# Sums of E and v of four tiles in one slot, heads visited 0 to 3 then 3 to 0 with four key buffers

## The chip, the cores and the metric

The kernel runs on one core of one Trainium2 chip. The metric is the device time of one execution in microseconds (us), lower is better. Before the change it is 1399.04 us, the median of 3 runs (1398.97 to 1399.08). The engines of a core run side by side, each through its own list of instructions, and wait for each other by semaphores: PE (matrix products; its weight loads stand as PEld), DVE (vector work), ACT (activations, copies out of PSUM), POOL (elementwise work on SBUF), SP (here it issues all DMAs).

## What is computed

Attention that keeps the 32 best keys of every query, and behind it a channel mix with the token before. In the reference, cut:

```python
# q, k, v: 8 batches, 8 heads, 576 tokens, 64 channels
scores = scale * np.matmul(q, k.transpose(0, 1, 3, 2))
kth = np.partition(scores, -32, axis=-1)[..., -32:-31]
scores = np.where(scores >= kth, scores, -1e9)
attn = np.exp(scores - scores.max(-1, keepdims=True))
attn = attn / (attn.sum(-1, keepdims=True) + 1e-09)
x = np.matmul(attn, v)            # heads side by side: 8, 576, 512
x_prev = ...                      # x, one token later
xk = mu_k * x + (1 - mu_k) * x_prev
xr = mu_r * x + (1 - mu_r) * x_prev
h = np.maximum(xk @ w_k, 0.0)     # 512 to 1024
out = sigmoid(xr @ w_r) * (h * h @ w_v)
```

## The kernel before

**Slots and visits.** Two heads lie side by side on the partitions as one pair (`hp`, four pairs a batch). A tile is 128 queries of one head against its 576 keys; a pair has nine tiles (the ninth holds the last 64 queries of both heads). The program is one long list of slots, one new tile a slot, 288 tiles in all; in one slot a tile gets its scores while older tiles are at later steps. `ORDER` gives the order of the steps within a slot, and it is the same in every slot. The tiles come in visits: for each batch the four pairs with tiles 0 to 3, then the four pairs again with tiles 4 to 8, each time in the order 0, 1, 2, 3.

**One tile.** In its own slot PE makes the scores (`ps`, L239; L243 for the ninth tile) and ACT copies them out (`keep`, L248). One slot later DVE looks for the best of seven pieces (`cand`, L272), two slots later it ranks them, ACT takes signs against a bound (L288) and POOL multiplies (L291), three slots later comes the threshold, exp (L299) and the masked E (L302). Four slots later PE transposes E (`turn_tile`, L318, and L328 for the last 64 keys) and ACT copies it out (`et`, `el`). Five slots later (`W = tiles[n - 5]`) comes `weigh`: the sums of E and v.

**The sums.** `weigh(g, U, u)` takes two tiles (one query block of both heads): eight products with `v_in` (L376) and two with `vr_in` (L378), and writes beside the scores in the same two PSUM banks. A unit `U` is four tiles. Before the change half u = 0 is weighed in the slot of the unit's second tile plus five, half u = 1 two slots later, when the unit is full; the ninth tile is weighed alone. In the slot of the full unit PE also transposes the inverse row sums (`turn_inverse`, L349), and one slot later DVE multiplies the sums by them into `xT` (`place`, L384, L389).

**Keys.** Each visit loads its keys by four DMAs (`load_keys`, tag `kt`, L179), turns them on PE by two groups of three transposes (`turn_k`, output `pk`, L208) and ACT copies each group out (`K`, L216), four and three slots ahead of the visit. `K` has two buffers. Queries come in the same way (`turn_q`: `pq`, L208, and `qs`, L211).

**The channel mix** is cut into pieces of twelve products (`ph`, `pz`, `pv`, L437 to L439; some have six), and a slot takes none, one or two of them in step `mix`, between `inv` and `weigh` on PE. How many is settled when the program is built, by a budget: each slot adds `PACE` = 4.60 to what is free on PE, at most `CAP` = 4.45, the steps take their planned costs off (`L.use("pe", ...)`), and a piece is placed while there is enough for it. Pieces also wait for tokens, that is for whole rows of `xT`. What is left over runs in slots behind the last tile.

```python
PACE, SHARE, PIECE, CAP, MOST = 4.60, 0.74, 1.52, 4.45, 2
            def inv():
                if W and (W.i % 2 or W.i == 8):
                    L.use("pe", 1.33 if W.i % 2 else 0.7)
            def weigh_():
                if W and (W.i % 2 or W.i == 8):
                    weigh(g, W.U, W.i // 2 % 2)
```

In the first some forty slots the weights of the channel mix are also loaded and split (`weight_block`), on DVE, ACT and POOL.

Of the kernel before, what the change touches and what calls it, by code (L numbers as in the profile page):

```python
# [21 lines left out]
HS = S // 2  # L22
# [10 lines left out]
NCH = 7  # L33
CUTS = [S * i // NCH for i in range(NCH + 1)]
# [10 lines left out]
def topk_attention_channel_mix(ctx: ExitStack, tc: tile.TileContext, q, k, v, mu_k, mu_r, w_k, w_v, w_r, out):  # L45
# [18 lines left out]
    el_hf = [consts.tile([128, 256], F32, name=f"el{i}") for i in range(2)]  # L64
# [31 lines left out]
    def weight_steps(g, L):  # L96

        blocks = [(w_r, wr, i, 0) for i in range(HP)]
        blocks += [(w_k, wk, i, c) for c in range(0, FF, 512) for i in range(HP)]
        blocks += [(w_v, wv, i, 0) for i in range(NFB)]  # L100
        for src, dst, i, c in blocks:
            weight_block(g, L, src[i * 128:(i + 1) * 128, c:c + 512], *(d[:, i, c:c + 512] for d in dst), half=dst is wv)
            yield
            yield

    def weight_block(g, L, block, hi, lo, half):
        val = g.one.tile([128, 512], U32, name="wval")
# [12 lines left out]
        st = g.one.tile([128, 512, 2], U32, name="wst")  # L120
        nc.sync.dma_start(st.rearrange("p c t -> p (c t)"), block.bitcast(U32))
# [3 lines left out]
        def magnitude():  # L125
            W.mag = g.one.tile([128, 512], U32, name="wmag")
            nc.scalar.activation(W.mag.bitcast(F32), high.bitcast(F32), AF.Abs)
# [72 lines left out]
    def new_k(g, P):  # L200
        P.K = g.two.tile([128, 2, HS], F32, name="K")
        P.qs = {}
# [107 lines left out]
    def turn_tile(g, T, L):  # L310
        U, i = T.U, T.i
        j, u = i % 2, i // 2 % 2
        if i % 4 == 0:
            U.et, U.el = {}, {}
        et = U.et[u, j] = g.two.tile([128, NKC, 128], F32, name=f"et{j}")
        pt = g.psT.tile([128, NKC, 128], F32, name="pt", tag="pm")
        for c in range(NKC):
            nc.tensor.transpose(pt[:, c, :], T.e[:, c * 128:(c + 1) * 128], ident)  # L318
        L.at(*EVAC, lambda: nc.scalar.activation(et, pt, AF.Copy))  # L319
        if i % 2 == 0:  # L320
            T.U.e0 = T.e
        if i % 2 or i == 8:
            es = (T.e,) if i == 8 else (T.U.e0, T.e)
            pl = extra(g)[:64, :len(es) * 128]
            el = U.el[u] = el_hf[g.turns % 2][:, :len(es) * 128]
# [328 lines left out]
    def prep_all(g, P, batch, hp, L):  # L654
        P.first, P.near = 0, False
# [27 lines left out]
    def new_batch(g):  # L683
        x = g.two.tile([128, HP, 1 + S], F32, name="xT")
        nc.vector.memset(x[:, :, 0:1], 0.0)
        return x

    def pipeline(g):
        L = Lanes()

        visits = [(b, hp, part) for b in range(B) for part in (range(4), range(4, 9)) for hp in range(HP)]
# [3 lines left out]
        where = [(p, i) for p, (*_, part) in enumerate(visits) for i in part]  # L695
        xT, tiles, state = {}, {}, {"tokens": 0, "wait": 0, "start": 0, "held": []}
# [62 lines left out]
        def new_pair(n):  # L759
# [3 lines left out]
            P.first, P.near = P.part[0], len(P.part) < 9  # L763
# [16 lines left out]
        while n < total + 7 or "next" in state or L.busy():  # L780
# [6 lines left out]
            def loads():  # L787
                for N, t in coming(n):
                    early = N.n > 1
                    if t == -5 or t == -4 and not early:  # L790
                        N.kt, N.qt = [load_keys(g, N.batch, N.hp, 0)], []
                    if t == -4:
                        N.kt.append(load_keys(g, N.batch, N.hp, 1))
                        if 8 in N.part:
                            N.rest = load_rest(g, N.batch, N.hp)
# [6 lines left out]
            def score():  # L802
                if n < total:
# [3 lines left out]
                    if i == P.first:  # L807
                        if p % HP == 0:
                            state["seen"] = g.two.tile([128, HP, 3, 9], F32, name="seen")
                        P.group, P.seen = state["seen"], state["seen"][:, p % HP]  # L810
# [15 lines left out]
            def inv():  # L826
                if W and (W.i % 2 or W.i == 8):
                    L.use("pe", 1.33 if W.i % 2 else 0.7)
# [15 lines left out]
            def weigh_():  # L844
                if W and (W.i % 2 or W.i == 8):
                    weigh(g, W.U, W.i // 2 % 2)

            def prep():
                for N, t in coming(n):
                    at = (-4, -3) if N.n > 1 else (-3, -2)  # L850
                    if t == at[0]:
                        new_k(g, N)
                    if t in at:
                        turn_k(g, N, at.index(t), L)
                    if t in (-2, -1):
                        turn_q(g, N, t + 2, L)
                    if t == 0 and 8 in N.part:
                        turn_rest(g, N, L)
                    if -4 <= t < 0:
                        L.use("pe", 0.35)  # L860
                        L.use("act", 0.4)
# [59 lines left out]
            def place_():  # L921
                T = tiles.get(n - 6)
                if T and ends(T):
                    U = T.U
                    if U.P.b not in xT:
# [4 lines left out]
                        xT[U.P.b] = new_batch(g)  # L930
                    U.xT = xT[U.P.b]
                    place(U)
                    if U.P.hp == HP - 1 and T.i == U.P.part[-1]:
                        state["tokens"] = U.P.b * S + (S if T.i == 8 else 256)
                if V and V.i == V.P.part[-1] and V.P.hp == HP - 1:
# [98 lines left out]
```

## Time and profile before

| | |
|---|---|
| median of 3 runs | 1399.04 us (1398.97 to 1399.08) |
| profiled execution, its own time | 1397.27 us |
| span of its instructions | 1395.5 us |
| PE busy | 1257.8 us, 90% |
| DVE busy | 1154.9 us, 83% |
| ACT busy | 1113.2 us, 80% |
| POOL busy | 910.3 us, 65% |
| HBM | 55 GB/s over the span |

The span runs from the first to the last instruction of the profiled execution; its own time is 1.8 us longer, and the median of the runs 1.8 us longer again. Busy time is time in which at least one instruction of the engine ran; a busy PE is not PE at its peak, since its products are pipelined. The shares are means over stages with different limits, so the rows below go by stages.

### The profile page before, as it was taken

To read this page: it belongs to the slowest core of one execution; us is meant where nothing else is said; L and a number is where in the kernel's file an instruction comes from. 1 tells how busy PE (TensorE), PEld (TensorE's weight loads), DVE (VectorE), ACT (ScalarE), POOL (GpSimd) and SP (SyncE) were. 2 spreads that over 40 slices of the span, in tenths; PEclk is the share of its full clock that TensorE was granted. 3 is DMA by queue.
4 is the path that set the end of the run, shared out by engine and by line. 5 is a ranking of instruction groups with operands and counts; after the bars stand their busy time and mean duration, and the time that the engine had idled before them with its cause. 6 is when DMAs were issued, how large, how long until landed. Compare 5 with 4: busy or idle time off the path is not lost.

```text
span 1395.5 us, 32734 instructions
## 1 busy us (share of the span) xinstructions
PE 1257.8 (90%) x9909; PEld 961.0 (69%) x9909; DVE 1154.9 (83%) x6448; ACT 1113.2 (80%) x2588; POOL 910.3 (65%) x839
## 2 busy tenths in 40 slices
PE   5665767999999999898999999999999998999997
PEld 3443645676867687675867787777868686768786
DVE  6999899888898888989888898888888889888400
ACT  5777877898888888879889898888888887888541
POOL 3657886567655855657658675776666656757562
PEclk9777997999999999999999999999999999999999
DMA  4333232222221222222221222122222122111000
GB/s 102 85 89 84 59 95 66 59 50 56 50 68 40 62 52 60 51 50 64 47 71 41 53 62 63 41 55 57 66 52 51 43 70 68 37 45 37 21 16 22
DMA packets 243815, 78.78 MB, mean 56 GB/s; under 512 B 236464, under 2 KB 236464, under 8 KB 243632
## 3 DMA queue, kind: packets, MB, share of 16 engines
q1 hardware_dynamic: 243632, 76.61, 22.7%
q8 instruction: 82, 1.34, 0.4%
q14 instruction: 101, 0.83, 0.2%
HBM read 67.11 MB, written 9.44 MB: 55 GB/s over the span
## 4 chain that ended last, share of the span: by engine, by line
PE 66%; DVE 14%; ACT 9%; POOL 7%; issue 2%; SPq 0%; DMA 0%; DVEq 0%; ACTq 0%; POOLq 0%
PE ps L239 9%; PE ps L376 8%; PE pt L318 8%; PE ph L438 5%; PE ph L437 5%; PE pv L439 5%; PE ph L439 5%; PE pv L437 4%; PE pv L438 4%; DVE E L302 2%; DVE cand L272 2%; POOL sg L291 2%; PE pz L437 2%; PE pz L439 2%; PE pz L438 2%
## 5 line engine op out<-in xcount | busy, mean ns | idle before, releaser
L291 POOL TENSOR_TENSOR sg<-sc,sg 128x576 f32<-128x576 f32 x288 | 413.8, 1437 | 413.7 <-ACT sg L288 345.4
L272 DVE MAX8 cand<-sc 128x8 f32<-128x82 f32 (+1 forms) x2016 | 469.9, 233 | 10.1 <-ACT sc L248 8.1
L248 ACT ACTIVATE sc<-ps 128x576 f32<-128x576 f32 x288 | 187.0, 649 | 155.8 <-PE ps L239 101.9
L910 DVE MAX8 top<-sg 128x8 f32<-128x576 f32 x288 | 218.1, 757 | 80.4 <-POOL sg L291 78.8
L239 PE MATMUL ps<-K,qs 64*128 64x288 f32 x1024 | 207.6, 484 | 48.8 <-DVE xT L384 28.7
L299 ACT ACTIVATE se<-sc,seen 128x576 f32<-128x576 f32 x288 | 213.9, 743 | 27.2 <-DVE wval L133 25.3
L302 DVE SCALAR_TENSOR_TENSOR E<-sc,seen,se 128x576 f32<-128x576 f32 x288 | 233.0, 809 | 0.9 <-PE ps L243 0.3
L288 ACT ACTIVATE sg<-sc,seen 128x576 f32<-128x576 f32 x288 | 222.1, 771 | 5.0 <-DVE seen L283 2.6
L318 PEld LDWEIGHTS pt<-ident,E 128*128 128x128 f32 x1152 | 126.3, 145 | 133.5 <-issue 92.0
L318 PE MATMUL pt<-ident,E 128*128 128x128 f32 x1152 | 196.9, 296 | 13.8 <-DVE E L302 11.9
L376 PE MATMUL ps<-et,v_in 128*64 128x128 f32 (+1 forms) x2560 | 174.5, 282 | 22.5 <-ACT sc L248 15.2
L376 PEld LDWEIGHTS ps<-et,v_in 128*64 128x64 f32 x2560 | 136.9, 145 | 65.0 <-ACT sc L248 20.9
L438 PE MATMUL ph<-xl,wk 128*128 128x256 f32 (+2 forms) x608 | 172.5, 284 | 8.5 <-POOL xl L433 8.5
L437 PE MATMUL ph<-xh,wk 128*128 128x256 f32 (+2 forms) x608 | 178.9, 294 | 1.5 <-ACT r L454 1.3
L275 DVE MAX8 top<-cand 128x8 f32<-128x56 f32 x864 | 177.0, 205 | 0.1
L319 ACT ACTIVATE et<-pt 128x512 f32<-128x512 f32 x288 | 169.4, 588 | 4.0 <-PE pt L318 4.0
L439 PE MATMUL ph<-xh,wk 128*128 128x256 f32 (+2 forms) x608 | 171.3, 282 | 0.0
L239 PEld LDWEIGHTS ps<-K,qs 64*128 64x128 f32 x1024 | 82.2, 196 | 104.4 <-issue 34.6
L439 PE MATMUL pv<-wv,hl 128*128 128x512 f32 (+1 forms) x296 | 118.5, 400 | 9.2 <-POOL hl L458 9.2
L437 PE MATMUL pv<-wv,hh 128*128 128x512 f32 (+1 forms) x296 | 125.5, 424 | 0.0
L438 PEld LDWEIGHTS ph<-xl,wk 128*128 128x128 f32 x608 | 116.6, 192 | 11.1 <-POOL xl L433 10.9
L437 PEld LDWEIGHTS ph<-xh,wk 128*128 128x128 f32 x608 | 116.3, 191 | 2.4 <-ACT r L454 1.6
(95 smaller groups left out, 2687.4 us busy)
## 6 DMA issues: line engine op xcount, KB each, us to landing
kt<-in_k SPq DMA_DIRECT2D x256, 72.0 KB, 2.2
q_near<-in_q SPq DMA_DIRECT2D x256, 64.0 KB, 2.1
v_in<-in_v SPq DMA_DIRECT2D x128, 128.0 KB, 2.5
out<-eb SPq DMA_DIRECT2D x35, 256.0 KB, 2.3
wst<-in_moe_w_k SPq DMA_DIRECT2D x8, 512.0 KB, 4.0
wst<-in_moe_w_v SPq DMA_DIRECT2D x8, 512.0 KB, 3.8
vr_in<-in_v SPq DMA_DIRECT2D x64, 32.0 KB, 2.3
wst<-in_moe_w_r SPq DMA_DIRECT2D x4, 512.0 KB, 4.0
```

The source lines that it names most:

```text
L239: nc.tensor.matmul(g.ps[:, e], lhsT=P.qs[j][h, c * 128:(c + 1) * 128], rhs=P.K[h, j], start=True, stop=True)
L272: nc.vector.max(T.cand[:, 8 * i:8 * i + 8], T.sc[:, CUTS[i]:CUTS[i + 1]])
L288: nc.scalar.activation(T.side, T.sc, AF.Sign, bias=T.under, scale=-BELOW, accum_out=T.cnt)
L291: nc.gpsimd.tensor_mul(T.side, T.sc, T.side)
L299: nc.scalar.activation(g.pe, T.sc, AF.Exp, bias=T.nb, scale=SCALE)
L302: nc.vector.scalar_tensor_tensor(T.e, T.sc, T.thr, g.pe, op0=OP.is_ge, op1=OP.mult, accum_out=T.rs)
L318: nc.tensor.transpose(pt[:, c, :], T.e[:, c * 128:(c + 1) * 128], ident)
L376: nc.tensor.matmul(pa[hs[j]], lhsT=P.v[:, j, c, :], rhs=ms[c][j], start=(c == 0), stop=False)
L437: nc.tensor.matmul(ps, lhsT=sh, rhs=mh, start=first, stop=False)
L438: nc.tensor.matmul(ps, lhsT=sh, rhs=ml, start=False, stop=False)
L439: nc.tensor.matmul(ps, lhsT=sl, rhs=mh, start=False, stop=last)
L910: nc.vector.max(M.top[:, 24:32], M.side)
```

## The change

- `weigh_` now acts only in the slot of a full unit (`last`), and then weighs both halves, one behind the other: twenty products in one slot where ten stood in each of two. The planned cost on PE goes from 1.33 in each of two slots to 2.5 in one. For that, the transposed E of the first tiles is held longer: `et` of even tiles has three buffers where it had two, `el` three where it had two.
- The second round of visits of a batch takes the pairs in the order 3, 2, 1, 0. `K` has four buffers of its own, and a visit whose pair is still held (`homes`, `N.own` false) takes that `K`: no loads, no transposes, no copies of keys in the second round.
- To make room, the working tiles of the weight loading become parts of one tile, `early`, in the place of the odd batches' `xT`.
- Where the code asked for the fourth pair it now asks for the last visit of a round (`P.last`).

The diff, cut to what the steps below speak of:

```diff
+KEYS = 4
-    el_hf = [consts.tile([128, 256], F32, name=f"el{i}") for i in range(2)]
+    el_hf = [consts.tile([128, 256], F32, name=f"el{i}") for i in range(3)]
...
+        g.early = g.one.tile([128, HP * (1 + S)], F32, name="early", tag="x1")
...
-        val = g.one.tile([128, 512], U32, name="wval")
+        val = g.early[:, 1024:1536].bitcast(U32)
...
     def new_k(g, P):
-        P.K = g.two.tile([128, 2, HS], F32, name="K")
-        P.qs = {}
+        P.K = g.one.tile([128, 2, HS], F32, name="K", tag=f"K{P.home}")
...
-        et = U.et[u, j] = g.two.tile([128, NKC, 128], F32, name=f"et{j}")
+        et = U.et[u, j] = (g.two if j else g.three).tile([128, NKC, 128], F32, name=f"et{j}")
...
-        visits = [(b, hp, part) for b in range(B) for part in (range(4), range(4, 9)) for hp in range(HP)]
+        visits = []
+        for b in range(B):
+            visits += [(b, hp, range(4)) for hp in range(HP)]
+            visits += [(b, hp, range(4, 9)) for hp in reversed(range(HP))]
...
+        homes, held = {}, [(-1, None)] * KEYS
+        for p, (b, hp, part) in enumerate(visits):
+            home = next((h for h, (_, of) in enumerate(held) if of == (b, hp)), None)
+            own = home is None
+            if own:
+                home = held.index(min(held, key=lambda x: x[0]))
+            held[home] = p, (b, hp)
+            homes[p] = own, home
...
+            P.own, P.home = homes[n]
+            if not P.own:
+                P.K = next(N.K for N in reversed(Ps.values()) if (N.b, N.hp) == (P.b, P.hp) and N is not P)
...
-                    if t == -5 or t == -4 and not early:
-                        N.kt, N.qt = [load_keys(g, N.batch, N.hp, 0)], []
+                    if N.own and (t == -5 or t == -4 and not early):
+                        N.kt = [load_keys(g, N.batch, N.hp, 0)]
                     if t == -4:
-                        N.kt.append(load_keys(g, N.batch, N.hp, 1))
+                        N.qt = []
+                        if N.own:
+                            N.kt.append(load_keys(g, N.batch, N.hp, 1))
...
             def inv():
-                if W and (W.i % 2 or W.i == 8):
-                    L.use("pe", 1.33 if W.i % 2 else 0.7)
+                if last:
+                    L.use("pe", 2.5 if W.i < 8 else 0.7)
...
             def weigh_():
-                if W and (W.i % 2 or W.i == 8):
-                    weigh(g, W.U, W.i // 2 % 2)
+                if last:
+                    for u in range(2 if W.i < 8 else 1):
+                        weigh(g, W.U, u)
...
-                    if t in at:
+                    if N.own and t in at:
                         turn_k(g, N, at.index(t), L)
+                        L.use("pe", 0.35)
+                        L.use("act", 0.4)
                     if t in (-2, -1):
                         turn_q(g, N, t + 2, L)
+                        L.use("pe", 0.35)
+                        L.use("act", 0.4)
                     if t == 0 and 8 in N.part:
                         turn_rest(g, N, L)
-                    if -4 <= t < 0:
-                        L.use("pe", 0.35)
-                        L.use("act", 0.4)
```

How the order of instructions moves, at three places. Line numbers of the changed program are one or two higher for the same code.

First, PE in the slot of the last tile but one of a visit in the second round of batch 5 (the scores of tile 204), before the change. `px` from E are the last 64 keys of E, `px` from `rb` is the inverse, `pq` are queries; the twelve rows of one mix piece are left out behind its first three.

```order
L239 MATMUL ps<-K,qs_14397 128x288 x2
L318 MATMUL pt<-ident,E 128x128 x4
L328 MATMUL px<-ident,E 64x128
L208 MATMUL pq<-ident,q_near 128x128 x2
L349 MATMUL px<-ident,rb 128x128 x2
L437 MATMUL ph<-xh,wk_66 128x256
L438 MATMUL ph<-xl,wk_66 128x256
L439 MATMUL ph<-xh,wk_67 128x256
...
L376 MATMUL ps<-et_14523,v_in 64x128
L376 MATMUL ps<-et_14612,v_in 64x128
...
L378 MATMUL ps<-el_76,vr_in 64x128 x2
```

The same slot of the changed program: no mix piece stands in it, and the sums of both halves follow the inverse directly.

```order
L240 MATMUL ps<-K,qs_13956 128x288 x2
L319 MATMUL pt<-ident,E 128x128 x4
L329 MATMUL px<-ident,E 64x128
L209 MATMUL pq<-ident,q_near 128x128 x2
L350 MATMUL px<-ident,rb 128x128 x2
L377 MATMUL ps<-et_13947,v_in 64x128
L377 MATMUL ps<-et_14019,v_in 64x128
...
L379 MATMUL ps<-el_75,vr_in 64x128 x2
L377 MATMUL ps<-et_14083,v_in 64x128
L377 MATMUL ps<-et_14158,v_in 64x128
...
L379 MATMUL ps<-el_76,vr_in 64x128 x2
```

The piece has moved to an earlier slot, where one half of the sums stood before.

Second, PE in the slot before (tile 203), before the change, up to the first product of the mix: the keys of the next visit, `pk`, are turned here.

```order
L239 MATMUL ps<-K,qs_14332 128x288 x2
L318 MATMUL pt<-ident,E 128x128 x4
L328 MATMUL px<-ident,E 64x128 x2
L208 MATMUL pk<-ident,kt_14534 128x96 x3
L437 MATMUL ph<-xh,wk_66 128x256
```

The same place after the change; the next visit is of a pair whose keys are held, and the mix follows the transposes of E at once.

```order
L240 MATMUL ps<-K,qs_13888 128x288 x2
L319 MATMUL pt<-ident,E 128x128 x4
L329 MATMUL px<-ident,E 64x128 x2
L438 MATMUL ph<-xh,wk_66 128x256
```

Third, SP's queue near the end, in the second round of the last batch, before the change: `v_in` and `vr_in` of a visit, then keys (`kt`), the ninth tile's queries (`qr_in`) and the near queries of the next one.

```order
L194 DMA v_in<-in_v 128x4x64 x2
L195 DMA vr_in<-in_v 64x2x64
L179 DMA kt_20127<-in_k 96x3x64 x2
L179 DMA kt_20193<-in_k 96x3x64 x2
L186 DMA qr_in<-in_q 64x64 x4
L173 DMA q_near<-in_q 128x2x64 x4
```

And after the change: the four key loads are gone from the queue, the rest stands in the same order.

```order
L196 DMA v_in<-in_v 128x4x64 x2
L197 DMA vr_in<-in_v 64x2x64
L188 DMA qr_in<-in_q 64x64 x4
L175 DMA q_near<-in_q 128x2x64 x4
```

## Rows read from the trace of the kernel before

**Rows 1.** The page: busy time, share of the span and number of instructions of each engine, and the busy share of PE, DVE and ACT in 40 equal slices of the span (9 is 90% or more), with the granted clock of TensorE in tenths.

```profile
PE 1257.8 (90%) x9909; PEld 961.0 (69%) x9909; DVE 1154.9 (83%) x6448; ACT 1113.2 (80%) x2588; POOL 910.3 (65%) x839
...
PE   5665767999999999898999999999999998999997
...
DVE  6999899888898888989888898888888889888400
ACT  5777877898888888879889898888888887888541
...
PEclk9777997999999999999999999999999999999999
```

**Rows 2.** Busy time of each engine in three stretches of the span: the first 45 slots, the other 243 slots that have a tile, and the slots behind the last tile. Columns: stretch, its length, busy us of PE, PEld, DVE, ACT and POOL with their instructions, mean granted clock, DMA share, GB/s.

```profile
0.00:245.00 245.00, 163.40 (x1098) 114.04 (x1098) 219.81 (x1079) 179.45 (x392) 166.84 (x151) 0.83 0.33 83
245.00:1293.00 1048.00, 1003.22 (x8202) 771.62 (x8204) 917.24 (x5300) 897.21 (x2112) 693.10 (x632) 0.99 0.23 54
1293.00:1395.50 102.50, 91.18 (x616) 75.35 (x616) 17.81 (x72) 36.52 (x86) 50.37 (x57) 0.98 0.07 20
```

**Rows 3.** The same columns for two short stretches: three slots with no mix piece, and eleven slots with one or two each.

```profile
706.80:718.70 11.90, 9.09 (x79) 6.67 (x78) 11.64 (x67) 10.77 (x25) 8.66 (x8) 0.86 0.36 89
1033.70:1082.00 48.30, 48.30 (x400) 38.45 (x399) 41.28 (x239) 40.36 (x91) 31.13 (x29) 1.00 0.21 49
```

**Rows 4.** Groups of instructions over the whole span: line, engine, operation, out<-in, shapes, number | busy us, mean ns of one | idle time of the engine before them and what ended it. The transposes of keys, their copy by ACT, and the products of E and v. The last row is from the page's list of DMA issues: KB each and us to landing.

```profile
L208 PE MATMUL pk<-ident,kt 96*128 96x96 f32 x384 | 56.4, 257 | 8.3 <-DMA kt<-in_k 6.3 <-ACT wmag L127 1.4 <-ACT sc L248 0.2
L216 ACT ACTIVATE K<-pk 128x288 f32<-128x288 f32 x128 | 51.8, 405 | 2.4 <-PE pk L208 2.4
...
kt<-in_k SPq DMA_DIRECT2D x256, 72.0 KB, 2.2
```

**Rows 5.** The timeline of PE over two slots of the full stretch: start us, length us, engine, line, operation, out<-in, number, and idle time before it (none here). The products of the mix pieces are left out up to the last of each run.

```profile
915.64 0.40 PE L439 MATMUL pv<-wv,hl 128*128 128x512 f32 x1
915.97 1.09 PE L376 MATMUL ps<-et,v_in 128*64 128x128 f32 x16
916.89 0.39 PE L378 MATMUL ps<-el,vr_in 128*64 128x128 f32 x4
917.21 0.76 PE L239 MATMUL ps<-K,qs 64*128 64x288 f32 x4
917.90 0.66 PE L318 MATMUL pt<-ident,E 128*128 128x128 f32 x4
918.39 0.38 PE L328 MATMUL px<-ident,E 128*64 128x128 f32 x2
918.61 0.27 PE L208 MATMUL pr<-ident,qr_in 128*128 128x128 f32 x1
...
921.28 0.40 PE L439 MATMUL pv<-wv,hl 128*128 128x512 f32 x1
921.61 0.76 PE L239 MATMUL ps<-K,qs 64*128 64x288 f32 x4
922.29 0.66 PE L318 MATMUL pt<-ident,E 128*128 128x128 f32 x4
922.79 0.41 PE L208 MATMUL pk<-ident,kt 96*128 96x96 f32 x3
...
924.36 0.28 PE L439 MATMUL ph<-xh,wk 128*128 128x256 f32 x1
924.57 1.09 PE L376 MATMUL ps<-et,v_in 128*64 128x128 f32 x16
925.49 0.39 PE L378 MATMUL ps<-el,vr_in 128*64 128x128 f32 x4
925.81 0.76 PE L239 MATMUL ps<-K,qs 64*128 64x288 f32 x4
```

**Rows 6.** The timeline of all engines over the three slots without a mix piece of rows 3, same columns, cut to the scores (L239), ACT's copy of them (L248), the sums (L376) and DVE's `place` (L384).

```profile
706.84 0.76 PE L239 MATMUL ps<-K,qs 64*128 64x288 f32 x4
...
707.72 0.65 ACT L248 ACTIVATE sc<-ps 128x576 f32<-128x576 f32 x1 [1.46 <-PE ps L239]
...
708.58 1.09 PE L376 MATMUL ps<-et,v_in 128*64 128x128 f32 x16
...
709.82 0.76 PE L239 MATMUL ps<-K,qs 64*128 64x288 f32 x4
...
713.65 0.43 DVE L384 TENSOR_TENSOR xT<-ps,ri 128x256 f32<-128x256 f32 x1
...
714.13 0.76 PE L239 MATMUL ps<-K,qs 64*128 64x288 f32 x4 [2.50 <-DVE xT L384]
...
715.68 0.64 ACT L248 ACTIVATE sc<-ps 128x576 f32<-128x576 f32 x1
...
716.37 1.98 PE L376 MATMUL ps<-et,v_in 128*64 128x128 f32 x16 [0.31 <-ACT sc L248]
...
718.68 0.76 PE L239 MATMUL ps<-K,qs 64*128 64x288 f32 x4
```

**Rows 7.** The two longest of PE's waits between 245 and 1293 us: engine, its tile and line, what it waited for: us in total, times, longest us.

```profile
PE ps L239 <- DVE xT L384: 10.4, 5, 2.7
PE ps L376 <- ACT sc L248: 9.8, 11, 1.5
```

More of the change, by code (lines that the diff above doesn't have):

```diff
@@ L119, in weight_block @@
             return
-        st = g.one.tile([128, 512, 2], U32, name="wst")
-        nc.sync.dma_start(st.rearrange("p c t -> p (c t)"), block.bitcast(U32))
+        st = g.early[:, :1024].bitcast(U32).rearrange("p (c t) -> p c t", t=2)
+        nc.sync.dma_start(g.early[:, :1024].bitcast(U32), block.bitcast(U32))
         low, high = st[:, :, 0], st[:, :, 1]
@@ L125, in magnitude @@
         def magnitude():
-            W.mag = g.one.tile([128, 512], U32, name="wmag")
+            W.mag = g.early[:, 1536:2048].bitcast(U32)
             nc.scalar.activation(W.mag.bitcast(F32), high.bitcast(F32), AF.Abs)
@@ L324, in turn_tile @@
             pl = extra(g)[:64, :len(es) * 128]
-            el = U.el[u] = el_hf[g.turns % 2][:, :len(es) * 128]
+            el = U.el[u] = el_hf[g.turns % 3][:, :len(es) * 128]
             g.turns += 1
@@ L654, in prep_all @@
     def prep_all(g, P, batch, hp, L):
-        P.first, P.near = 0, False
+        P.first, P.near, P.home, P.qs = 0, False, 0, {}
         new_k(g, P)
@@ L681, in prep_first, with new_batch @@
         return lambda: half(1)
-    def new_batch(g):
-        x = g.two.tile([128, HP, 1 + S], F32, name="xT")
+    def new_batch(g, b=0):
+        x = g.one.tile([128, HP, 1 + S], F32, name="xT", tag=f"x{b % 2}")
         nc.vector.memset(x[:, :, 0:1], 0.0)
@@ L762, in new_pair @@
             P.b, P.hp, P.part = visits[n]
-            P.first, P.near = P.part[0], len(P.part) < 9
+            P.first, P.near, P.qs = P.part[0], len(P.part) < 9, {}
+            P.last = n % HP == HP - 1
+            P.own, P.home = homes[n]
+            if not P.own:
+                P.K = next(N.K for N in reversed(Ps.values()) if (N.b, N.hp) == (P.b, P.hp) and N is not P)
             P.batch = lambda x, b=P.b: x[b]
@@ L809, in score @@
                             state["seen"] = g.two.tile([128, HP, 3, 9], F32, name="seen")
-                        P.group, P.seen = state["seen"], state["seen"][:, p % HP]
+                        P.group, P.seen = state["seen"], state["seen"][:, P.hp]
                     if i % 4 == 0:
@@ L850, in prep @@
                     at = (-4, -3) if N.n > 1 else (-3, -2)
-                    if t == at[0]:
+                    if N.own and t == at[0]:
                         new_k(g, N)
-                    if t in at:
+                    if N.own and t in at:
                         turn_k(g, N, at.index(t), L)
+                        L.use("pe", 0.35)
+                        L.use("act", 0.4)
                     if t in (-2, -1):
                         turn_q(g, N, t + 2, L)
+                        L.use("pe", 0.35)
+                        L.use("act", 0.4)
                     if t == 0 and 8 in N.part:
                         turn_rest(g, N, L)
-                    if -4 <= t < 0:
-                        L.use("pe", 0.35)
-                        L.use("act", 0.4)
             def norm():
@@ L929, in place_ @@
                             L.force(g.read)
-                        xT[U.P.b] = new_batch(g)
+                        xT[U.P.b] = new_batch(g, U.P.b)
                     U.xT = xT[U.P.b]
                     place(U)
-                    if U.P.hp == HP - 1 and T.i == U.P.part[-1]:
+                    if U.P.last and T.i == U.P.part[-1]:
                         state["tokens"] = U.P.b * S + (S if T.i == 8 else 256)
-                if V and V.i == V.P.part[-1] and V.P.hp == HP - 1:
+                if V and V.i == V.P.part[-1] and V.P.last:
                     o = slice(V.P.first, V.i + 1)
```

## The prediction

> **What bounds the kernel now.** I begin with the busy shares and the slices of the page [rows 1]. PE leads with 90%, but its slices stand at 5 to 7 tenths for the first seventh of the span, while DVE's are full there, and at 9 after it. So I cut the span in three [rows 2]. In the first 245 us (45 slots, in which the weights are split) DVE is busy 219.8 and PE 163.4: PE is not the limit. From 245 to 1293 us (the other 243 slots with a tile) PE is busy 1003.2 of 1048.0, DVE 917.2, ACT 897.2. Behind that PE works off what is left of the mix.
>
> In the middle there are two kinds of stretch [rows 3]. Where slots hold mix pieces PE is busy 48.30 of 48.30 us, at full clock, and DVE 41.28. Where they hold none, DVE is busy 11.64 of 11.90 us and PE waits: three slots, so 3.88 us of DVE a slot. The timeline shows the first kind [rows 5]: the scores of successive tiles start at 917.21, 921.61 and 925.81, and what lies between is PE work without a gap. What a group costs PE is its end less the end of the group before it: scores 0.69, four transposes of E 0.59, the last keys' two 0.21, the transposes of keys 0.25 (922.79 + 0.41 against 922.29 + 0.66), two mix pieces 2.80 (918.88 to 921.68), one half of the sums 1.24 (916.04 to 917.28). They add up to the 4.40 and 4.20 us of the two slots. The second kind [rows 6]: slots of 2.98, 4.31 and 4.55 us, in which PE waits 2.50 us for `place`.
>
> So a slot costs about the larger of its PE work and DVE's 3.88. I put the group costs on the order of the program before, slot by slot. The 243 slots hold 980 us of PE work; taking 3.88 for every lighter slot gives 1038. The trace has 1048. The 10 left over I put down to the clock: its mean is 0.99 in that stretch [rows 2], and 1% missing at half speed is some 20 us at 1.2 GHz, in which up to half is lost. It shows in rows 6: after the wait of 2.50 us the sums take 1.98 where they took 1.09, and the granted clock of that stretch is 0.86 [rows 3].
>
> **The change part by part.**
>
> *Keys turned once.* 64 of 128 groups of transposes go, by the order 8 of 23 in the first 45 slots and 56 of 105 in the middle. A group costs PE 0.25 at least, and 56.4 us over 128 groups, 0.44, at most [rows 4], where nothing beside it overlaps; in a full stretch rows 5 are the case, and I take 0.26, which with the rest of the costs comes nearest to the slots. That is 56 x 0.26 = 14.6 us off PE in the middle. In the first 45 slots the 2 us off PE lie under DVE: 0, and 2 as a bound. ACT loses 64 copies of 0.405 us, 26 us [rows 4]; in full stretches ACT is busy 40.36 of 48.30 and hides them [rows 3], in light ones they could help DVE's chain a little: 0, bound 1. On SP 128 loads with 2.2 us to landing go [rows 4]; what stood behind them (queries, `qr_in`) is issued sooner, which nobody waits for in rows 7. The new `K` waits for the last scores of the pair that had its buffer, four visits back: 0.
>
> *Both halves of the sums in one slot.* The same twenty products run, 2 x 1.24 us, so nothing comes off. The first half moves two slots later on PE, past the scores, transposes and pieces of two slots; it issues no DMA. `et` and `el` have the buffers for it by the order (the third one is free when the next unit writes), and `place` still comes one slot after the second half. What was one slot of 4.2 and one of 4.5 becomes one with the sums and no piece (0.69 + 0.59 + 0.11 for one short transpose, 0.21 each for the pairs of the queries and the inverse, and 2.48: 4.29) and one with two pieces.
>
> *The mix.* By the order, 301 pieces stand in the middle before and 300 after, and 57 and 58 behind the last tile. Tokens come in the same slots, since the last visit of a round still ends the same slot. So the mix goes no earlier, and the work taken off PE partly becomes lighter slots. I did the same addition for the changed order: PE work 964 us (14.6 for the keys, 1.4 for the piece), and with 3.88 for each lighter slot 1029. Of the 16.0 us 7.0 are lost to slots in which DVE is the limit (58 us of such filling before, 65 after), and **9.0 us** come off.
>
> *The tail* has one piece more, 1.4 us, on a PE that is busy 91.18 of 102.50 us there: +1.4.
>
> *The clock.* By the order, runs of three or more slots in a row with less than 3.7 us of PE work number eight before and one after, which should leave fewer long waits; but single slots are down to 1.3 to 1.7 us after. Of the 10 us I take 1.5 as gained; bounds 0 and 10.
>
> *`early` in the place of `xT`.* By the order the last weight block is done in slot 41, and the tile of batch 1 is first written in slot 45: 0. If that cover were gone, `place` would wait on DVE for some slots, once.
>
> Sum: -9.0 + 1.4 - 1.5 = -9.1 us. The profiled execution took 1397.3 us by its own time (span 1395.5), and would take 1388.2; the median of the runs lies 1.8 above it, so **1390**.
>
> **The rivals.**
>
> *A: the idle time takes all of it.* The budget a slot (4.60) is unchanged, so full slots stay as long and the mix is only done sooner in each chunk. For it: 7 of 16 us go that way in my own sum. Against it: full slots have less in them (4.29 in the slots with sums, where they had up to 4.5). It gives 1399 + 1.4 - 1.5, within 0.2% of before (0.2%, 2.8 us, is about what a measurement of this kernel can tell from no change).
>
> *B: slower, by a wait of the sums for `keep`.* The sums write the banks from which ACT copies the scores, so they wait for that copy of the same slot [rows 7]. Before, a mix piece of 1.4 us mostly stood between. By the order 54 double sums stand right behind the inverse now, before only 21 single ones did. 11 waits took 9.8 us, 0.89 each [rows 7]. If as large a part of the 54 waits (28), that is 25 us: 1390 + 25 = 1415. It decides from 13 waits on (11.8 us, the gain and 0.2%). Behind a waiting product stand the next scores, and for them ACT and DVE. Against it: in rows 6 the copy of the scores that started at 706.84 ends at 708.37, 1.53 later, and the sums come 1.74 after them without a wait; the wait comes only where ACT was late itself (715.68, 1.55 after the scores), in a light stretch. The double sums stand at 1.8 in full ones. The Trainium skill (PSUM — Partial Sum Buffer, "PSUM bank collisions raise a hardware error") says that two engines may not touch one bank in the same partitions at once, whatever the columns, so this wait can't be dropped; the trace agrees, as these products do wait for a copy of other columns.
>
> *C: slower, by the clock.* The order after has 28 separate light runs where it had 22. In rows 6 a drop costs the sums 716.37 to 718.75, 2.38, instead of 1.24: 1.1 us and more. If each of the 28 brought one, 31 us instead of 10: 1412. Against it: PE falls to half in the rows only after a wait of 2.5 us, and single light slots are bridged, since DVE is ahead after full slots (41.28 of 48.30). The Trainium skill (TensorE: Matmul & The Clock Gate, "HAM oscillation — how this bites in real kernels") tells of just this: bursts with idle gaps between them start at half clock each time, which would make shorter, more frequent gaps a danger. Rows 3 and 6 agree that a gap is followed by half clock; how many of the new gaps are long enough no row shows.
>
> *D: more gain.* All 64 groups count, the filling doesn't grow and the half-clock time goes: -16.6 + 1.4 - 10, with the ACT bound 1373.
>
> **How the numbers follow.** The forecast (1383 to 1396) has 0.62, D 0.12, A 0.14, B 0.09, C 0.03. The range is to leave out B and C and the lower half of D: 1378 to 1400. Faster is the forecast and D, with a little added for A's lower edge: 0.75; same 0.14; slower B and C, 0.11.
>
> **What would show it.** `pk` x192 and `K` x64 in the groups; 28 us less of PE's summed products. From 245 us on, the last tile's scores about 9 us sooner. PE's busy time some 16 us less, its idle time some 6 more, most of it before scores that wait for `place`. The row of the sums waiting for `keep` should stay under 15 us; over 25 us means B. A mean clock under 0.98 in the middle means C. If the middle's slots start as late as before although PE is busy 15 us less, it is A. The prediction is wrong as a whole if full slots turn out longer than the sum of their groups, that is if three slots in a row with two pieces make ACT the late one.

## The result and the profile after

The changed kernel takes 1367.18 us, the median of four runs (1365.87 to 1370.06), against 1399.06 for the kernel before beside it: a ratio of 0.977, interval 0.976 to 0.979. That is 31.9 us off where 9 were forecast, and below the range. Both profiled executions can be compared line by line: 1397.3 us before (span 1395.5) and 1367.4 after (span 1365.6), 29.9 us apart. Of the other 2 us, 1.8 are the distance of the kernel before's profiled execution from its median.

The shares of the page after and the three stretches that answer to [rows 2], cut where slot 45 and the last tile start (columns as there):

```profile
PE 1229.5 (90%) x9717; PEld 947.6 (69%) x9717; DVE 1150.9 (84%) x6448; ACT 1096.0 (80%) x2524; POOL 908.5 (67%) x840
...
0.00:243.00 243.00, 164.78 (x1101) 115.80 (x1101) 222.33 (x1087) 179.86 (x389) 168.60 (x153) 0.82 0.32 78
243.00:1264.00 1021.00, 972.99 (x8002) 755.23 (x8004) 911.75 (x5299) 880.59 (x2051) 690.49 (x633) 0.99 0.20 47
1264.00:1365.60 101.60, 91.70 (x622) 76.54 (x621) 16.81 (x64) 35.56 (x84) 49.40 (x55) 0.98 0.07 20
```

The start is 5 us shorter (slot 45 begins at 242.9 instead of 247.8), the middle 24 (1020.9 instead of 1045.1, both from slot 45 to the last tile's scores), the tail 1. The groups that answer to [rows 4] and the waits that answer to [rows 7] (total us, times, longest):

```profile
L209 PE MATMUL pk<-ident,kt 96*128 96x96 f32 x192 | 28.7, 261 | 5.8 <-DMA kt<-in_k 5.2 <-ACT r L455 0.5
L217 ACT ACTIVATE K<-pk 128x288 f32<-128x288 f32 x64 | 25.9, 405 | 2.4 <-PE pk L209 2.4
...
PE ps L240 <- DVE xT L385: 10.7, 7, 2.1
PE ps L377 <- ACT sc L249: 7.0, 9, 1.3
```

Turns and copies of keys are halved as the diff says, and the sums wait less for `keep` than before, not more. Where the middle's 24 us went, by adding up PE's rows group by group (what each adds to the end of the one before it):

```
slots 45 to 287, us             before   after
PE work, all groups             1000.3   972.9
  transposes of keys              27.7    12.6
  sums                           158.9   151.9
  mix pieces (301, then 300)     432.6   427.3
PE waiting                        44.8    48.0
of it all, at 1.2 GHz             27.3    23.9
```

The keys are as forecast. The sums fell by 7 us though every product is still there (3200 rows of them in either trace). The timeline of PE in a slot with both halves, to be read against the single halves of [rows 5] (start us, length us, engine, line, operation, out<-in):

```profile
932.92 0.38 PE L350 MATMUL px<-ident,rb 128*128 128x128 f32 x2
933.23 1.09 PE L377 MATMUL ps<-et,v_in 128*64 128x128 f32 x16
934.16 0.39 PE L379 MATMUL ps<-el,vr_in 128*64 128x128 f32 x4
934.38 1.04 PE L377 MATMUL ps<-et,v_in 128*64 128x128 f32 x16
935.25 0.39 PE L379 MATMUL ps<-el,vr_in 128*64 128x128 f32 x4
935.57 0.72 PE L244 MATMUL ps<-K,qr 64*64 64x288 f32 x8
```

From a half's last group to what follows it takes 0.22 us where another half follows (934.16 to 934.38) and 0.32 where scores follow (935.25 to 935.57; in rows 5, 916.89 to 917.21). Over the slots of the middle at full clock the median half adds 1.243 us before, two side by side 2.334: 0.152 less than twice one half. What is saved is the way into the sums, not the way out: the scores behind them add 0.685 us (the median), and behind a mix piece 0.685 too.

### The profile page after: what moved, and what is told of

Its sections match the earlier page's. It is cut to its first block, busy times and chain, and to the rows that moved or that the text cites. A ratio compares the mean times of both kernels' runs of the same rounds, so it can differ in the third digit from the quotient of the medians.

```text
span 1365.6 us, 32014 instructions
## 1 busy us (share of the span) xinstructions
PE 1229.5 (90%) x9717; PEld 947.6 (69%) x9717; DVE 1150.9 (84%) x6448; ACT 1096.0 (80%) x2524; POOL 908.5 (67%) x840
## 4 chain that ended last, share of the span: by engine, by line
PE 65%; DVE 16%; ACT 10%; POOL 6%; issue 2%; SPq 0%; DMA 0%; DVEq 0%; ACTq 0%; POOLq 0%
PE ps L240 9%; PE ps L377 8%; PE pt L319 8%; PE ph L439 5%; PE ph L438 5%; PE ph L440 5%; PE pv L440 5%; PE pv L438 4%; PE pv L439 4%; DVE cand L273 3%; DVE E L303 3%; POOL sg L292 2%; ACT sg L289 2%; ACT sc L249 2%; PE pz L440 2%; PE pz L438 2%
## 5 line engine op out<-in xcount | busy, mean ns | idle before, releaser
L377 PEld LDWEIGHTS ps<-et,v_in 128*64 128x64 f32 x2560 | 142.9, 146 | 36.7 <-ACT sc L249 20.8
```

The costliest lines, as they stand in the source:

```text
L377: nc.tensor.matmul(pa[hs[j]], lhsT=P.v[:, j, c, :], rhs=ms[c][j], start=(c == 0), stop=False)
```

## The experiments

All times are medians, and each ratio is to the kernel before, measured beside it (1399.5 to 1400.8).

**The parts alone.** The first run keeps the visits and key buffers of the change and has the sums, their plan and their buffers as before (`weigh` at every odd tile). The second is the kernel before with the reverse of this edit, and the change's third `et` and `el`.

```
-                if last:
-                    for u in range(2 if W.i < 8 else 1):
-                        weigh(g, W.U, u)
+                if W and (W.i % 2 or W.i == 8):
+                    weigh(g, W.U, W.i // 2 % 2)
```

> The changed kernel, but the sums stand as before the change: one half in the slot of the second tile plus five, the other two slots later, two buffers for et and el. Theory (the missing 23 us have several places: 9 from the two halves standing side by side on PE, 5 in the first 45 slots, 7 of filling that did not grow): the keys give about 17 us of PE work and most of the 5 at the start, so 1377 to 1382. Rival (the whole gain is ACT's and PE's relief by the keys): 1367 to 1370.

> The kernel before with the sums alone changed: both halves in the slot of the full unit, three buffers for et of even tiles and for el; visits and keys as before. Theory (side by side the two halves cost 2.33 us and not 2.49, since PE changes the shape of its array once less each way): 9 to 10 us less, 1389 to 1391, and together with the keys alone the 32 us within 5. Rival (moving the sums gives nothing by itself, or costs by waits for ACT's copy of the scores): 1397 to 1405.

Keys alone: 1378.5 (0.984, 0.982 to 0.986). Sums alone: 1383.7 (0.989, 0.987 to 0.992), 5 to 7 us better than expected. The early gain belongs to the sums, not to the keys as the first expectation had it: slot 45 starts at 242.4 with the sums alone and at 248.1 with the keys alone. By the profiled executions the two gains (18.7 and 15.6) overlap by some 4 us. That lies in the tail: with the keys alone 304 pieces, not 300, fit into the middle, and the tail is 6.4 us shorter than before; with both it is 0.9 shorter.

**What putting the halves side by side is worth.** Two transposes of the identity stand between the two halves (first, shown here), or ahead of both (second):

```
                 if last:
+                    if W.i < 8:
+                        pd = g.psM.tile([128, 512], F32, name="pd", tag="pm")
                     for u in range(2 if W.i < 8 else 1):
                         weigh(g, W.U, u)
+                        if W.i < 8 and u == 0:
+                            for c in range(2):
+                                nc.tensor.transpose(pd[:, c * 128:(c + 1) * 128], ident, ident)
```

> The changed kernel with two extra 128x128 transposes (of the identity, into a spare PSUM tile) between the two halves of the sums, 64 times. Theory (each change of PE between full products and products of 64 columns costs about 0.08 us): the sums cost 2 x 1.24 again, so 64 x (0.22 + 0.15) = 24 us of PE work more, 1385 to 1391, and 8 to 10 us above the run with the same transposes ahead of both. Rival (the 0.15 us is not of the neighbours): no difference between the two runs.

> The changed kernel with the same two extra transposes ahead of both halves, behind the inverse's. Theory: the sums stay at 2.33 us, 64 x 0.22 = 14 us of PE work more, 1377 to 1381. Rival: as with the transposes between the halves, 1385 to 1391.

1393.1 (0.996, 0.994 to 0.997) and 1406.8 (1.004, 1.003 to 1.006). As times both missed. In the first PE has 27.8 us more to do in the middle: the sums are back at 158.9 us, as before the change, and the transposes take 20.6 where 14 were expected. In the second they take 17.4, but the middle grows by 40.4, and the row of waits names why, the PSUM buffer that they take:

```profile
PE pd L867 <- ACT et L320: 27.5, 24, 2.4
```

So the two totals can't be set against each other, but the groups can: a half adds 1.243 again where something stands between, and two add 2.334 where the same transposes stand ahead of them. One place of the first run, on PE:

```profile
950.73 0.39 PE L379 MATMUL ps<-el,vr_in 128*64 128x128 f32 x4
951.05 0.44 PE L870 MATMUL pd<-ident 128*128 128x128 f32 x2
951.42 1.09 PE L377 MATMUL ps<-et,v_in 128*64 128x128 f32 x16
```

Here the two transposes add 0.37 us (951.12 to 951.49; the median is 0.368), and 0.218 where they stand ahead of the sums. So the step out of the sums costs them 0.150, as the step in costs the sums 0.152. The theory of that run had 0.08 a step, about half of that.

**The keys' turns and copies put back into the changed kernel**, in the slots where they stood, without a plan for them: three transposes of the identity a half (first), ScalarE's copy of them to a spare tile too (second), and keys loaded, turned and copied in every visit (third; `own = True`).

```
+                    if not N.own and t in at:
+                        pd = g.psM.tile([128, MAIN], F32, name="pk", tag="pm")[:, :HS]
+                        for c in range(KB):
+                            nc.tensor.transpose(pd[:, c * KP:(c + 1) * KP], ident[:KP], ident[:KP, :KP])
+                        L.at(0, "high", lambda pd=pd: nc.scalar.activation(spare, pd, AF.Copy))
```

The first has not the last line.

> The changed kernel, with three transposes of the identity for each half of the keys that a visit no longer turns, in the slots where these turns stood, into a buffer of the same PSUM pool and read by nobody (no copy, no load, nothing planned for them, so the order of everything else is that of the changed kernel). 64 groups of turns that cost TensorE 18.2 us over the program (38.0 us before, 19.8 after). Theory (the keys' gain is TensorE's own time and nothing else): the whole of it comes back, 1367 + 18 = 1385, between 1381 and 1388. Rival (the gain is ScalarE's copies and the loads that went with the turns, or is hidden in slots where TensorE waits anyway): +9 or less, up to 1376.

> The run before this one, and ScalarE copies each such group into a spare tile that nobody reads. Theory (ScalarE is not on the path; its copies fit where it waits): 0 to 2 us over the run with the turns alone, 1383 to 1390. Rival (ScalarE's relief is part of the gain): 5 us or more over the run with the turns alone.

> The changed kernel with keys loaded, turned and copied in every visit again (the new order of visits, four key buffers and the sums in one slot stay, and the plan counts what the changed kernel counts). By the run with turns and copies back (1383.0) the loads are the only thing more. Theory (loads are hidden, 0.23 against 0.19 of the DMA engines' time): 1382 to 1385. Rival (the loads delay others): 1387 or more. The run with the sums alone, which differs from this one by the order of visits and the plan, took 1383.7.

1377.0 (0.984, 0.981 to 0.987), 1383.0 (0.987, 0.985 to 0.990), 1383.0 (0.989, 0.988 to 0.991). The theory was wrong about the make-up: PE's turns are worth 10 us of the 18 expected, though PE is 17 us busier with them (1246.8 against 1229.5), and ScalarE's copies another 6, which it had at nothing. A copy also holds one of the four PSUM buffers for longer; no run tells this from ScalarE's time. Between those two runs no single place stands out; the middle grows by 5.5 us, 4.3 of it in slots right behind those with a copy. Why is left open. Together 15.8 us is what the keys are worth when they are put back into the changed kernel (alone on the kernel before they gave 22); the loads add 0 to 3 (medians, ratios), as expected.

**The start.** The kernel before, with its first gate and first hidden piece held back:

```
             now = next(ins, None)
+            if not (g.gates if which else g.hiddens):
+                for _ in range(1 if which else 1):
+                    yield 1
             yield from (gates if which else hiddens)(c, x)
```

> The kernel before with one thing changed: the first gate piece and the first hidden piece of the mix are held back one slot (slot 25 in place of 24, and 30 in place of 28), nothing else about the sums or keys. In the kernel before, TensorE stands still 4.1 and 4.6 us there for POOL's low half of the mixed inputs (xl); in the run with the sums alone it doesn't. Theory (the 5 us that the changed kernel gains before slot 45 come from this shift alone): 1399 to 1394, between 1393 and 1396, with slot 45 starting at 242 to 244 us instead of 247.8. Rival (the 5 us come from the sums' work itself or from other waits): 1398 to 1400 and slot 45 at 247 to 248.

1394.3 (0.996, 0.995 to 0.997): 5 to 6 us by medians and 3.8 by the profiled executions, the theory's side, though slot 45 starts at 244.5, not quite as early as in the changed kernel. In the kernel before PE waits here, twice, between 100 and 248 us:

```profile
PE ph L438 <- POOL xl L433: 4.6, 1, 4.6
PE pz L439 <- POOL xl L433: 4.1, 1, 4.1
```

Both rows are gone with the pieces held back, with the sums alone and in the changed kernel. In the last two the double sums are booked into slots 24 and 29, so the first pieces find no room until POOL is done; in all three they stand in slots 25 and 30. Two other runs bear this out. With the keys alone, and with three pieces of sums in a slot (below), the first pieces stand in slots 24 and 28 as before, PE waits there again (4.8 and 3.5 us, 4.3 and 3.5 us), and slot 45 starts at 248.1 and 247.7.

**The ninth tile's sums into the same slot.** The sums of tiles 4 to 7 wait one slot and run with the ninth tile's, and are placed with it:

```
-                if last:
-                    for u in range(2 if W.i < 8 else 1):
-                        weigh(g, W.U, u)
+                if last and W.i != 7:
+                    for U, u in ([(W.U, 0), (W.U, 1)] if W.i < 8 else [(W.before, 0), (W.before, 1), (W.U, 0)]):
+                        weigh(g, U, u)
```

> The changed kernel with the sums of tiles 4 to 7 one slot later, together with those of the ninth tile: three pieces of sums in one slot, so 32 times less that TensorE goes into the sums and out of them (their placing into xT moves with them). Theory (0.15 us saved for each pair of sums laid side by side, and light slots cost nothing more than their work): 32 x 0.15 = 4.8 us less than the changed kernel, 1362, between 1358 and 1366; the sums' time falls by 4 to 5 us in the trace. Rival (the prediction's way: a slot with less work than VectorE's 3.88 us is filled up with waiting): counted over the slots of this order, 1042 us against 1021, so 20 us more of waiting, 1367 - 5 + 20 = 1382.

1406.9 (1.006, 1.004 to 1.007), slower than both said. The saving is in the rows: three pieces add 2.920 us, where two and one added 2.334 and 0.732, again 0.146 less for one step less into the sums, 4.7 us for 32. But PE waits 19 us more in the middle (its first rows below), and 61.4 us run at 1.2 GHz there instead of 23.9, about 19 us lost. The 5 us of the start are lost again too.

```profile
PE ps L377 <- ACT sc L249: 13.3, 15, 1.5
PE px L350 <- POOL rb L344: 10.3, 11, 1.3
PE pt L319 <- DVE top L276: 9.1, 8, 1.5
```

**Work where PE waits, and where it doesn't.** Twelve transposes of the identity behind the 20 slots of the middle without pieces and sums (first; `done == 0`), or behind 20 full ones (second; every fifth with `done == 2`):

```
-                work(MOST)
+                done = work(MOST)
+                if 45 <= n < 288 and not last and done == 0:
+                    pd = g.psM.tile([128, 512], F32, name="pd", tag="pm")
+                    for c in range(12):
+                        nc.tensor.transpose(pd[:, c % 4 * 128:(c % 4 + 1) * 128], ident, ident)
```

> The changed kernel with 12 transposes of the identity (4 of them take about 0.59 us in a tile's turn, so some 1.76 us) at the end of each of the 20 slots between 45 and 287 that hold no sums and no mix piece; order and plan of everything else unchanged. 35 us of TensorE work in all. The prediction's way (a slot takes at least VectorE's 3.88 us, so work in a light slot is free up to there; these slots hold 1.6 us and would hold 3.4): 0 to 3 us, 1367 to 1370. Theory (TensorE comes into a light slot late from the full ones before it and VectorE's slack is shared over neighbours: in the changed kernel's trace these slots pass in 2.5 us, so only 0.9 us of each is waiting): 35 - 20 x 0.9 = 17 us, 1384, between 1379 and 1390.

> The same 20 groups of 12 transposes, at the end of 20 slots that hold two mix pieces and no sums (every fifth such slot). Both ways expect the full price here, since TensorE is the bound in these slots: 35 us, 1402; if neighbouring light slots take some of it up (theory), 28 to 35 us, 1395 to 1402. Under 25 us would say that waiting is spread over all slots alike.

In full slots: 1393.2 (0.996, 0.994 to 0.997), 26 us for 26.2 us of added work, the full price (a group adds 1.3 us, not the 1.76 expected). In light slots: **1361.2** (0.973, 0.971 to 0.974), 6 us faster than without. Neither side expected that. Two light slots of the changed kernel and the slot behind them, on PE (last column: idle time before it and what ended it):

```profile
468.44 0.76 PE L240 MATMUL ps<-K,qs 64*128 64x288 f32 x4
469.12 0.66 PE L319 MATMUL pt<-ident,E 128*128 128x128 f32 x4
469.99 0.76 PE L240 MATMUL ps<-K,qs 64*128 64x288 f32 x4 [0.21 <-ACT sc L249]
471.87 0.63 PE L319 MATMUL pt<-ident,E 128*128 128x128 f32 x4 [1.13 <-DVE top L276]
...
473.22 0.76 PE L240 MATMUL ps<-K,qs 64*128 64x288 f32 x4 [0.50 <-ACT sc L249]
475.25 1.11 PE L319 MATMUL pt<-ident,E 128*128 128x128 f32 x4 [1.27 <-DVE E L303]
...
477.84 1.98 PE L377 MATMUL ps<-et,v_in 128*64 128x128 f32 x16 [0.17 <-ACT sc L249]
```

and the same slots with the added work:

```profile
467.18 0.76 PE L240 MATMUL ps<-K,qs 64*128 64x288 f32 x4
467.87 0.66 PE L319 MATMUL pt<-ident,E 128*128 128x128 f32 x4
468.36 1.47 PE L926 MATMUL pd<-ident 128*128 128x128 f32 x12
469.76 0.76 PE L240 MATMUL ps<-K,qs 64*128 64x288 f32 x4
...
471.24 1.47 PE L926 MATMUL pd<-ident 128*128 128x128 f32 x12
472.64 0.76 PE L240 MATMUL ps<-K,qs 64*128 64x288 f32 x4
474.10 0.63 PE L319 MATMUL pt<-ident,E 128*128 128x128 f32 x4 [0.70 <-DVE top L276]
...
476.58 1.09 PE L377 MATMUL ps<-et,v_in 128*64 128x128 f32 x16 [0.41 <-ACT sc L249]
```

Each with its stretches (columns as in rows 2), first the changed kernel:

```profile
470.00:475.00 5.00, 2.35 (x14) 1.20 (x14) 5.00 (x28) 4.31 (x11) 4.15 (x6) 1.00 0.42 115
475.00:482.00 7.00, 6.58 (x49) 5.69 (x49) 6.38 (x43) 6.39 (x16) 7.00 (x10) 0.51 0.00 0
```

```profile
470.00:475.00 5.00, 4.29 (x33) 3.06 (x31) 5.00 (x34) 4.38 (x11) 4.92 (x7) 1.00 0.33 96
475.00:479.00 4.00, 2.90 (x47) 2.44 (x50) 4.00 (x27) 4.00 (x11) 4.00 (x7) 1.00 0.02 4
```

In the changed kernel PE is busy 2.35 of 5 us, and then runs at 0.51 of full speed, the lower level, so the sums take 1.98 instead of 1.09. With the added work it is busy 4.29 of the 5, and the clock stays at the upper level. Over the middle: 26.6 us of work more, 21.9 us of waiting less, 20.5 us at 1.2 GHz less (3.4 instead of 23.9), worth about 10: 26.6 - 21.9 - 10.3 = -5.6. The middle went from 1020.9 to 1016.0, the start gave 0.9. Light slots with 1.59 us of work pass in 2.52 us in the changed kernel (the mean), and with 2.92 in 3.10.

**The pace, and the same on the kernel before.** TensorE's credit a slot at 4.0 instead of 4.60 (first), that and the work in light slots (second); then the kernel before with work in its 10 light slots (third) and with the slower pace (fourth):

```
-                self.free[lane] = min(self.free[lane] + PACE, CAP)
+                self.free[lane] = min(self.free[lane] + (4.0 if lane == 'pe' else PACE), CAP)
```

> The changed kernel with the credit that TensorE's lane is given per slot at 4.0 in place of 4.60, so that pieces are spread more evenly and three more are left for the tail. Counted over the slots of this order with 3.88 us as a slot's least and 1.41 us for each piece in the tail, 1098.5 against 1101.1: the prediction's way expects 2.6 us less, 1364.6. Theory (a light slot costs 0.9 us of waiting, not 2.3): the three pieces more in the tail cost 3 x 1.41 = 4.2 us and are taken from full slots at the same price, so no change beyond 2 us, 1366 to 1369.

> The changed kernel with TensorE's credit at 4.0 (1356.1 alone) and 12 transposes of the identity in each of its 15 slots without sums and pieces (1361.2 alone with 20 such slots). Theory (TensorE's waiting in light slots lets the clock fall to 1.2 GHz, and the full slots behind pay for it; 17.1 us of half clock are left between slots 45 and 287 in the run with the slower pace): another 3 to 8 us less, 1348 to 1353, with less than 6 us of half clock there. Rival (the two runs gained by the same thing, so little is left): 1355 to 1358.

> The kernel before with 12 transposes of the identity at the end of each of its 10 slots between 45 and 287 that hold no sums and no mix piece, 17 us of TensorE work by the plan, 13 us by the trace of the like run (1.33 us a slot). In the kernel before these slots pass in 3.2 us with 1.7 us of work, and 27.3 us run at half clock. Theory (waiting in light slots costs by the clock too): half clock falls to less than half and the time by 3 to 8 us, 1391 to 1396. Rival (the kernel before was held by its full slots and by the order of its sums alone): 1399 to 1412.

> The kernel before with TensorE's credit at 4.0, as in the run of the changed kernel that took 1356.1. Counted over slots (3.88 us at least, 1.41 for a piece in the tail) 1115.1 against 1109.9: the prediction's way expects 5 us more, 1404. Theory (what is taken out of full slots comes back in full, and waiting in light slots is cheaper than that count has it): within 4 us of before, 1396 to 1402; if it gains 8 us or more here too, the gain of the slower pace has nothing to do with the change.

1356.1 (0.969, 0.967 to 0.971), 1354.7 (0.967, 0.966 to 0.969), 1389.8 (0.992, 0.991 to 0.994) and 1376.8 (0.983, 0.981 to 0.984). The slower pace alone beat every expectation, by at least 8 us in the changed kernel and 19 in the kernel before. The middle of the changed kernel with the slower pace (first fence), of the changed kernel with work in light slots at the old pace (second), and of the kernel before with work in its light slots (third; columns as in rows 2):

```profile
244.00:1246.50 1002.50, 964.96 (x7976) 748.81 (x7972) 910.40 (x5301) 876.21 (x2047) 686.60 (x628) 0.99 0.20 48
```

```profile
242.00:1258.00 1016.00, 989.86 (x8238) 773.82 (x8236) 911.21 (x5301) 879.95 (x2051) 689.67 (x632) 1.00 0.20 47
```

```profile
249.00:1286.00 1037.00, 1004.23 (x8294) 774.42 (x8290) 914.28 (x5288) 893.52 (x2105) 691.60 (x631) 1.00 0.23 54
```

With the slower pace (first fence) PE works 965.0 of 1002.5 us: 8 us less work, as three pieces moved to the tail, which grew by 6.4, and 17.1 us run at 1.2 GHz instead of 23.9; and 10.5 us less waiting. That is 11 us faster with no idle work at all, the version to keep. Work in its light slots adds nothing that can be told from it: the two are mostly one gain, near the rival's 1355 to 1358. The kernel before pays for its light slots too (third fence: clock 1.00, 3.4 us at 1.2 GHz instead of 27.3), 10.8 us by medians and 7.4 by the profiled executions. So this price stood in both kernels and is next to no part of the change. The slower pace helps the kernel before by 24 us by medians and 16 by profiles. At that pace the change is worth some 20 us, at the old one 32.

## Why the prediction was wrong

*The keys*: near in size, -14.6 against -15.8 when put back (and -22 alone), but not in kind. PE's turns gave 10 of their 17 us; ScalarE's copies, "0, bound 1", gave 6.

*The sums, "the same twenty products run, 2 x 1.24 us, so nothing comes off"*: this step failed. Side by side they are 2.33, and the whole program's sums fell from 199.3 to 190.3 us, 9.0 less. Rows 5 had a sign of it: sixteen products of a half pass in 0.92 us (915.97 to 916.89), so twenty would in 1.15, and the half was counted as 1.24. I took 1.24 as the work of a half, when it held the step into the sums. The runs with something between the halves and ahead of them, and the three pieces at 2.92, agree. The Trainium skill (TensorEngine Tiling (Array Packing), "Key Properties") says that a change of tiling mode, not of the tile, drains TensorE. The rows are in line with it, but no run here shows that it is the mode: a step costs 0.15 us into the sums (128*64), out of them into 128*128 transposes, and from the scores (64*128) into those of E (four add 0.587 there, where two elsewhere add 0.218), while the two `px` transposes of 128*64 behind 128*128 ones add 0.218, so no step. The prediction left steps between groups out.

*The start, priced at nothing*: -4.9 us. I read there only that DVE was busy. The two waits for `xl`, 8.7 us, lay on the path, and the new booking passed them by. Holding two pieces back alone gave 5 to 6 us.

*"7.0 are lost to slots in which DVE is the limit"*: failed. PE's waiting grew by 3.2 us and half clock fell by 3.4 (1.7 lost less), so 1.5 net. A slot isn't the larger of its own work and 3.88: PE reaches a single light slot late, from full ones of 4.2 to 4.5 us in which DVE gained 0.3 to 0.6 each, and the 20 lightest pass in 2.52 us. My own argument against C ("single light slots are bridged") said so, and the sum didn't use it. That its terms for the kernel before (980 us of work, 58 of filling, 10 for the clock) added up to the 1048 of the trace was luck: that trace has 44.8 of waiting, and 1000.3 of work with the clock's part in it, so the filling was 13 too high and the rest 10 too low. The same count was wrong by more on the slower pace: +5 for the kernel before, where 16 to 24 came off.

*The tail*: one piece more, as said, but 0.9 us shorter instead of 1.4 longer (PE 91.70 against 91.18): 2.3. *The mix pieces* fell by 5.3 us where the piece and the clock gave 2.9. The cause of these two stays open.

By the profiles: 29.9 - 9.1 = 20.8 us missed, of them sums 7.0 (the middle's part), start 4.9, filling 3.8 in waiting, tail 2.3, pieces 2.4, keys 0.5.

*Rivals.* B did not come: 9 waits of 7.0 us, although the double sums stand right behind the inverse. C did not either, but its mechanism is real: in the run with three pieces it cost as much as the waiting, some 19 us each. A fell with the result. D (1373) came nearest in number, not in mechanism: PE's waiting did grow, and 23.9 of the 27.3 us at 1.2 GHz stayed; it lacked the sums and the start.

## What to carry to other kernels

Price a group by what it adds to the end of the one before, and ask how much of that belongs to the step into it: two halves of the sums were 0.15 us cheaper side by side than apart. A minimum per slot fitted a run of light slots here and not single ones, so a count of max(work, minimum) needs a test of its parts, work and waiting, and on a second order, before it is trusted. Where the bounding engine pauses now and then, look at what it pays afterwards: on the kernel before, spreading the work more evenly was worth about as much (16 to 24 us) as turning the keys once (19 to 22).

## What the runs showed of the hardware

More TensorE work made the program faster: 26.6 us of transposes nobody reads, put where it waited, took 6 us off, as the granted clock stayed at 2.4 GHz (3.4 us at 1.2 GHz in the middle instead of 23.9); on the kernel before 13.6 us of them took 7 to 11 off. And a step into the sums from other work of PE cost 0.146 to 0.152 us wherever it was measured, a step out of them into 128*128 transposes 0.150.
